# One core, attention inside a gMLP block: the row of score maxima is transposed one step sooner, and its DMA stands one or two steps sooner in the sync queue

## The chip, the cores and the metric

The kernel runs on 1 core of one Trainium2 chip. The metric is the device time of one execution in microseconds (us). A core has a matrix engine (PE, with PEld for its weight loads), a vector engine (DVE), a scalar engine (ACT), GpSimd (POOL) and a sync engine (SP), which here issues nearly all DMAs, in a fixed order.

## What is computed

All data is float32. A pre-norm attention layer with 32 heads of 20 numbers, in which each of 2048 positions sees itself and the 255 before it, is followed by a gMLP block:

```python
def _A_ref(x, wqkv, wo):
    B, S, D = x.shape                       # 1, 2048, 640
    H = 32; Dh = D // H; W = 256
    ...
    scores = jnp.einsum("bhqd,bhkd->bhqk", q, k) * (Dh ** -0.5)
    mask = (idx[:, None] - idx[None, :] >= 0) & (idx[:, None] - idx[None, :] < W)
    scores = jnp.where(mask[None, None], scores, -1e9)
    p = _softmax(scores, axis=-1)
    o = jnp.einsum("bhqk,bhkd->bhqd", p, v)
    return o.transpose(0, 2, 1, 3).reshape(B, S, D) @ wo
def _B_ref(x, w_in, w_sp, b_sp, w_out):
    z = _gelu(x @ w_in); z1 = z[..., :864]; z2 = _layernorm(z[..., 864:])
    g = jnp.einsum("ts,bsf->btf", w_sp, z2) + b_sp[None, :, None]
    return (z1 * g) @ w_out
h  = x + _A_ref(_layernorm(x), A_wqkv, A_wo)
h2 = h + _B_ref(_layernorm(h), B_w_in, B_w_sp, B_b_sp, B_w_out)
```

## The kernel before

The change lies in the attention loop, about 248 to 480 us into the span. Ahead of it stand the first layernorm and the q, k and v products; behind it the output projection and the gMLP block, which reaches to the end.

The 32 heads are eight groups of four, called 0 to 7 here. Queries and keys of a group, split in three bf16 parts, lie in a "stack", a slot of on-chip memory with one row for each part of each of 20 numbers (rows 0 to 119). There are three slots in rotation; their tiles are `slot` and `xb` (`slot_0`, `slot_1`, `xb_0`, `xb_1` for the two halves of the positions). `load_stack` fills a slot from DRAM (`slot<-qk_d`, L279).

The softmax needs the largest score of each query. The kernel works in two passes over the key and query blocks of 128:

- `max_item` (L300 on PE, L312 on DVE) computes the scores of one query block and one head with the query on the partition, and DVE takes the row maximum into a column of `mcol`.
- `score_item` (L366 on PE, L369 on ACT) computes the scores again with the key on the partition, with 123 rows in the product: rows 120 to 122 hold minus the maximum of each query, in three bf16 parts. ACT takes the exponential into `pt`, POOL cuts off the window's edges (L371, L374), and `pv_item` (L394) multiplies by the values. The result leaves PSUM by ACT (L408) or DVE (L410) into `ot`, and SP stores it (`o_d<-ot`, L411).

Between the passes the maxima have to become rows. `max_rows(g, b)` does it for group g and set b, in three pieces. Set 0 is query blocks 0 to 9, set 1 is blocks 10 to 15. The first piece splits the columns in three parts on POOL (L321 to L324, tile `m`). The second multiplies them by minus the identity on PE, which transposes them, and copies the result to `mt` on DVE. The third sends `mt` by DMA to rows 120 to 122 of the group's slot:

```python
            yield
            ps = s1_tile()[:3 * n, :P]
            nc.tensor.matmul(ps, m3.rearrange("p a c -> p (a c)"), minus, start=True, stop=True)   # L330
            mt = tmp2.tile([3 * n, P], BF16, tag="mt", bufs=1, name=f"mt{g}_{b}")
            nc.vector.tensor_copy(mt, ps)                                                          # L332
            yield
            nc.sync.dma_start(st[b][0][120:123], mt.bitcast(F32))                                  # L334
            yield
```

The loop goes over steps s = 0 to 129. A step takes one key block of the score pass, and the maxima of the block 17 places further on (`u1 = s + LEAD`, LEAD = 17), so that the maxima of a group are computed while the scores of the one before are. Within a step the four heads hh = 0 to 3 alternate; `pv_item(s - 2)` has its two halves at hh = 1 and hh = 3. The instructions of PE, DVE and ACT go out in exactly the order in which this code is written; those of SP also, from s = 0 to s = 112. POOL's order, and SP's outside that stretch, is set by a scheduler. Score products of a group begin at u1 % 16 = 1 and read the rows of set 0; those of set 1 are first read eight steps later.

`next(rows)` runs the next piece of `max_rows`. In the kernel before, the first piece stands at u1 % 16 = 10 for set 0 and at 0 for set 1, the second three steps later at hh = 1, and the third at the start of the step two steps after that. SP does nothing but issue DMAs in order, so a DMA stands behind all that were written ahead of it, and waits while one of these waits.

Of the kernel before, what the change touches and what calls it, by code (L numbers as in the profile page):

```python
# [20 lines left out]
NT = S // P  # L21
# [13 lines left out]
def block_kernel(ctx, tc, x, wqk, wv, wo, w_in, wsp, bsp, w_out, out):  # L35
# [5 lines left out]
    def pool(stack, name, **kw):  # L41
        return stack.enter_context(tc.tile_pool(name=name, bufs=1, reuse_waits="tile", **kw))
# [56 lines left out]
    def open_early(pl):  # L99
        mem["t1"] = pl.tile([P, 2 * KF * D], F32R, name="t1")  # L100
        mem["m1"] = pl.tile([P, 6 * D + 4 * P], F32, name="m1")
        mem["xh"] = [pl.tile([P, D], F32, name=f"xh{i}") for i in range(2)]
        mem["ho"] = [pl.tile([P, D], F32, name=f"ho{i}") for i in range(3)]
        mem["wraw"] = pl.tile([P, 2, 2, HF], F32, name="wraw")
# [55 lines left out]
    def proj_o(i, ps):  # L160
        osp = ots.pop(i)
        wo_s = t1(0, 2, KD, D)
        gemm(ps, HD, [lambda k, p=p: osp[:, p, k, :] for p in range(2)],
             [lambda k, j, p=p: wo_s[:, p, k, j * HD:(j + 1) * HD] for p in range(2)], KD)
        return ps
# [35 lines left out]
    with ExitStack() as ab:  # L201
# [43 lines left out]
        NU = 128  # L245
# [22 lines left out]
        def load_stack(g):  # L268


            st = slot_w[g % 3]
            if g < 3:
                for h in st:
                    nc.gpsimd.memset(h[1][96:P], ONES)
            for c in range(2):
                for j, parts in enumerate(((0, 0), (0, 1), (0, 2), (1, 0), (1, 1), (2, 0))):
                    for a in range(2):
                        src = qk_d[c][a][g // 4, parts[a], :, g % 4 * 4:g % 4 * 4 + 4]
                        nc.sync.dma_start(st[c][a][j:6 * DH:6], src)  # L279
                        yield  # L280
# [6 lines left out]
        def max_item(g, qb, hh, strips=True):  # L287

            st, half = slot_ap[g % 3], qb // 8
            ps = s1_tile()  # L290
            lo = max(0, qb - 2) * P
            n = (qb + 1) * P - lo
            keep = mask[:, 384 - n:]
            if strips:
                skip = 32 if qb > 1 else 0
                if skip:
                    n, keep = 288, strip
                for j in range(4):
                    q0 = qb * P + 32 * j
                    nc.tensor.matmul(ps[32 * j:32 * j + 32, :n], part(st, half, 120, 0, hh, q0, 32),  # L300
                                     part(st, half, 120, 1, hh, lo + skip * j, n),
                                     start=True, stop=True, tile_position=(0, 32 * j))
            else:
                nc.tensor.matmul(ps[:, :n], part(st, half, 120, 0, hh, qb * P, P), part(st, half, 120, 1, hh, lo, n),
                                 start=True, stop=True)
            b, c = (0, qb) if qb < 10 else (1, qb - 8)
            r = (10, 8)[b]
            if c == 2 * b and hh == 0:
                m_cols[b] = tmp2.tile([P, 4 * r], F32, tag=f"mcol{b}", bufs=1, name=f"mcol{g}_{b}")
            junk = tmp2.tile([P, 384], BF16, tag="junk", bufs=2, name=f"junk{g}_{qb}_{hh}")  # L310
            c += hh * r
            nc.vector.tensor_tensor_reduce(out=junk[:, :n], in0=ps[:, :n], in1=keep, scale=1.0,  # L312
                                           scalar=NEG, op0=OP.add, op1=OP.max, accum_out=m_cols[b][:, c:c + 1])

        def max_rows(g, b):


            n, cols, st = (40, 32)[b], m_cols.pop(b), slot_w[g % 3]
            m3 = tmp2.tile([P, 3, n], BF16, tag="m3", bufs=1, name=f"m3_{g}_{b}")
            mr = tmp2.tile([P, n], F32, tag="mr", bufs=1, name=f"mr{g}_{b}")  # L320
            nc.gpsimd.tensor_copy(out=m3[:, 0], in_=cols)  # L321
            nc.gpsimd.tensor_tensor(out=mr, in0=cols, in1=m3[:, 0], op=OP.subtract)
            nc.gpsimd.tensor_copy(out=m3[:, 1], in_=mr)
            nc.gpsimd.tensor_tensor(out=m3[:, 2], in0=mr, in1=m3[:, 1], op=OP.subtract)  # L324
            if b == 0:
                nc.gpsimd.tensor_copy(out=m_cols[1].rearrange("p (h r) -> p h r", h=4)[:, :, :2],
                                      in_=cols.rearrange("p (h r) -> p h r", h=4)[:, :, 8:])
# [8 lines that stand above are left out]
# [17 lines left out]
        def score_item(u, hh):  # L353


            g, kb = divmod(u, NT)
            st = slot_ap[g % 3]
            n = min(384, S - kb * P)
            if hh == 0:
                p_tiles[u] = tmp3.tile([P, 4, 384], F32, tag="pt", bufs=4, name=f"pt{u}")  # L360
            pt = p_tiles[u]
            ps = s2_tile()
            for i in range(4):
                k0, half = kb * P + 32 * i, kb // 8
                b, e = 32 * i, min(n, 32 * i + 288)
                nc.tensor.matmul(ps[32 * i:32 * i + 32, b:e], part(st, half, 123, 1, hh, k0, 32),  # L366
                                 part(st, half, 123, 0, hh, kb * P + b, e - b),
                                 start=True, stop=True, tile_position=(0, 32 * i))
            nc.scalar.activation(pt[:, hh, :n], ps[:, :n], AF.Exp, scale=SCALE)  # L369
            if hh == 3:  # L370
                nc.gpsimd.affine_select(out=pt[:, :, :P], in_=pt[:, :, :P], pattern=[[0, 4], [1, P]], base=0,  # L371
                                        channel_multiplier=-1, compare_op=OP.is_ge, fill=0.0)
                if n == 384:
                    nc.gpsimd.affine_select(out=pt[:, :, 256:], in_=pt[:, :, 256:], pattern=[[0, 4], [-1, P]],  # L374
                                            base=-1, channel_multiplier=1, compare_op=OP.is_ge, fill=0.0)
# [233 lines left out]
        for s in range(NU + 2):  # L609
            if s % NT == 0 and s < 6 * NT:  # L610
                ld = load_stack(s // NT + 2)
            u1 = s + LEAD
            if u1 <= NU + 5 and u1 % NT in (5, 15):
                next(rows)
            for _ in range(1 + s % 2):
                next(ld, None)
            for hh in range(4):
                if u1 < NU:
                    max_item(u1 // NT, u1 % NT, hh)
                if s < NU:  # L620
                    score_item(s, hh)
                if hh == 0 and u1 <= NU and u1 % NT in (0, 10):
                    rows = max_rows((u1 - 1) // NT, 0 if u1 % NT else 1)
                    next(rows)
                if hh == 1 and u1 <= NU + 3 and u1 % NT in (3, 13):
                    next(rows)
                if hh == 2 + s - NU and s >= NU:
                    if s == NU:
                        psB.close()
                        psW = pool(psB, "psW", space=PSUM)  # L630
                    pre_ps.append(proj_o(s - NU, psW.tile([P, 2, 512], F32, tag="wo", bufs=3, name=f"wo_ps{s - NU}")))
                if s >= 2:
                    if hh == 1:
                        pv = pv_item(s - 2)
                        next(pv, None)
                    if hh == 3:
                        next(pv, None)
            if u1 == NU:
                ring[2].append(ring[1].pop(0))
            if s == NU - NT:  # L640
                sync.close()
                low0.close()
                lowx.close()
                open_early(pool(early_stack, "early"))
                early = proj_early()
            if early is not None and s > NU - NT:
                next(early, None)
            for f in inverse:
                next(f, None)
# [566 lines left out]
```

## Time and profile before

| | |
|---|---|
| median of 3 runs | 1154.88 us (1151.7 to 1155.35) |
| the profiled execution | 1156.74 us, span 1154.3 us, mean granted clock 0.99 |
| PE busy | 1098.6 us (95% of the span), 10652 instructions |
| DVE, ACT, POOL busy | 746.3, 535.8, 406.1 us |
| chain that ended last | PE 31%, DVE 5%, POOL 2% of the span |
| L330, L332, L334 | 16 of each; medians 257, 286 and 757 ns |

The profile is one execution. PE is busy in almost the whole span, so what counts is where it is idle and what ended that. In rows of the timeline the columns are start (us from the span's start), length (us), engine, line, operation, tiles and count; behind them in brackets the idle time before, with what ended it. SP is written SPq there. A row of the waits gives the waiting engine, its tile and line, what it waited for, and the sum in us, the number and the longest. Window rows give, for each stretch, its length and the busy us of each engine with the number of its instructions, then the granted clock, the DMA engines' busy share and GB/s.

### The profile page before, as it was taken

What the parts mean: (1) busy time and instruction counts of PE and PEld (TensorE: products, weight loads), DVE (VectorE), ACT (ScalarE), POOL (GpSimd) and SP (SyncE); (2) the same over time, 40 slices, a digit from 0 to 9 for tenths busy, and PEclk for the clock granted to TensorE, in tenths of its full rate; (3) what the DMA queues carried; (4) which work ended last, traced back from release to release, by engine and by line L of the source; (5) the groups of instructions that cost most, each with busy time, mean ns of one, the idle gap of its engine ahead of it and who ended that gap; (6) DMA issues with size and microseconds to landing.
All of it is one profiled execution on the core that took longest, in us unless ns stands there. A gap on an engine that the chain in (4) does not pass through costs nothing. (4 is left out here: it accounts for less than half of the span.)

```text
span 1154.3 us, 27630 instructions
## 1 busy us (share of the span) xinstructions
PE 1098.6 (95%) x10652; PEld 982.7 (85%) x10652; DVE 746.3 (65%) x1963; ACT 535.8 (46%) x1165; POOL 406.1 (35%) x553
## 2 busy tenths in 40 slices
PE   6999999999999999889999998999999899999998
PEld 6998876667777776588999997999999799999998
DVE  5541113788999996789868489555548974655443
ACT  3333333258888889534356555333335421222210
POOL 4124444556667667656421065000116520000000
PEclk9999999999999999999999998999999999999999
DMA  6213565655666644487745412133341463444322
GB/s 194 69 35 98 169 209 173 213 182 185 192 193 199 192 155 147 151 256 269 255 143 206 157 50 74 68 120 131 103 137 52 145 199 135 133 144 133 97 80 81
DMA packets 83844, 170.84 MB, mean 148 GB/s; under 512 B 11008, under 2 KB 47360, under 8 KB 79872
## 3 DMA queue, kind: packets, MB, share of 16 engines
q1 hardware_dynamic: 81408, 163.83, 44.0%
q10 hardware_dynamic: 2304, 5.24, 1.2%
q8 instruction: 83, 1.36, 0.5%
q14 instruction: 49, 0.40, 0.1%
HBM read 112.37 MB, written 56.23 MB: 146 GB/s over the span
## 5 line engine op out<-in xcount | busy, mean ns | idle before, releaser
L369 ACT ACTIVATE pt<-bank 128x384 f32<-128x384 f32 (+2 forms) x512 | 201.6, 499 | 25.6 <-PE bank L300 11.6
L1013 PE MATMUL g<-zl,aw 128*128 128x432 f32 x768 | 174.5, 362 | 7.3 <-ACT zl L681 5.0
L681 ACT ACTIVATE aw<-fx 128x512 fp32r<-128x512 f32 (+2 forms) x160 | 92.8, 595 | 189.8 <-PE g L1013 124.2
L312 DVE CUSTOM_DVE_ANT_0 junk<-bank,strip 128x288 bf16<-128x288 f32 x392 | 157.4, 454 | 7.7 <-PE bank L300 5.2
L1013 PEld LDWEIGHTS g<-zl,aw 128*128 128x128 f32 x768 | 144.8, 189 | 16.2 <-ACT zl L681 5.9
L1013 PE MATMUL g<-ze,aw 128*128 128x432 f32 x576 | 138.1, 368 | 4.7 <-DVE row L675 2.4
L675 DVE TENSOR_TENSOR aw<-fx,aw 128x512 fp32r<-128x512 f32 (+2 forms) x152 | 107.8, 718 | 37.6 <-ACT aw L681 37.2
L394 PE MATMUL pv<-pt,v_sb 128*32 128x192 f32 (+3 forms) x1984 | 126.9, 323 | 2.4 <-POOL pt L371 1.9
L1013 PEld LDWEIGHTS g<-ze,aw 128*128 128x128 f32 x576 | 109.3, 192 | 12.6 <-DVE row L675 1.9
L366 PE MATMUL bank<-slot 123*32 123x288 bf16 (+6 forms) x1536 | 108.0, 283 | 10.3 <-DMA slot<-mt 8.7
L371 POOL TENSOR_SCALAR_AFFINE_SELECT pt<-pt 128x512 f32<-128x512 f32 x128 | 84.0, 657 | 60.2 <-ACT pt L369 59.7
L1052 PE MATMUL out_ps<-wout,y_sp 128*128 128x320 f32 (+1 forms) x630 | 96.2, 309 | 0.4 <-ACT y_sp L124 0.4
L1052 PEld LDWEIGHTS out_ps<-wout,y_sp 128*128 128x128 f32 (+1 forms) x630 | 94.1, 188 | 1.3 <-ACT y_sp L124 0.7
L917 PE MATMUL zb<-win,aw 128*128 128x432 f32 x480 | 95.2, 359 | 0.0
L917 PEld LDWEIGHTS zb<-win,aw 128*128 128x128 f32 x480 | 90.0, 188 | 4.5
L300 PE MATMUL bank<-slot 120*32 120x288 bf16 (+2 forms) x1264 | 88.3, 283 | 0.5 <-issue 0.5
L498 DVE TENSOR_TENSOR rest<-qk,sg 128x512 f32<-128x512 f32 x40 | 27.7, 692 | 86.9 <-ACT sg L496 86.8
L366 PEld LDWEIGHTS <-slot 123*32 123x32 bf16 x1536 | 53.0, 97 | 29.0 <-DMA slot<-mt 10.4
L501 POOL TENSOR_TENSOR sg<-rest,sg 128x512 bf16<-128x512 f32 x40 | 46.6, 1164 | 73.6 <-ACT sg L500 70.5
L374 POOL TENSOR_SCALAR_AFFINE_SELECT pt<-pt 128x512 f32<-128x512 f32 x112 | 72.3, 645 | 0.0
L675 DVE TENSOR_TENSOR row<-g,row 128x432 f32<-128x432 f32 x80 | 48.0, 603 | 36.7 <-PE g L1013 32.8
L394 PEld LDWEIGHTS pv<-pt,v_sb 128*32 128x32 f32 x1984 | 59.7, 110 | 8.4 <-POOL pt L371 3.8
(189 smaller groups left out, 2173.4 us busy)
## 6 DMA issues: line engine op xcount, KB each, us to landing
fx<-wsp_in SPq DMA_DIRECT2D x32, 512.0 KB
slot<-qk_d SPq DMA_DIRECT2D x72, 200.0 KB
qk_d<-sg SPq DMA_DIRECT2D x32, 384.0 KB
slot<-qk_d SPq DMA_DIRECT2D x72, 160.0 KB
fx<-hn_d SPq DMA_DIRECT2D x32, 320.0 KB
o_d<-ot SPq DMA_DIRECT2D x64, 128.0 KB
z_d<-row SPq DMA_DIRECT2D x16, 432.0 KB
g_d<-row SPq DMA_DIRECT2D x16, 432.0 KB
```

The source lines that it names most:

```text
L300: nc.tensor.matmul(ps[32 * j:32 * j + 32, :n], part(st, half, 120, 0, hh, q0, 32), part(st, half, 120, 1, hh, lo + skip * j, n), start=Tru ...
L312: nc.vector.tensor_tensor_reduce(out=junk[:, :n], in0=ps[:, :n], in1=keep, scale=1.0, scalar=NEG, op0=OP.add, op1=OP.max, accum_out=m_cols ...
L366: nc.tensor.matmul(ps[32 * i:32 * i + 32, b:e], part(st, half, 123, 1, hh, k0, 32), part(st, half, 123, 0, hh, kb * P + b, e - b), start=T ...
L369: nc.scalar.activation(pt[:, hh, :n], ps[:, :n], AF.Exp, scale=SCALE)
L371: nc.gpsimd.affine_select(out=pt[:, :, :P], in_=pt[:, :, :P], pattern=[[0, 4], [1, P]], base=0, channel_multiplier=-1, compare_op=OP.is_ge ...
L374: nc.gpsimd.affine_select(out=pt[:, :, 256:], in_=pt[:, :, 256:], pattern=[[0, 4], [-1, P]], base=-1, channel_multiplier=1, compare_op=OP. ...
L394: nc.tensor.matmul(ps[32 * hh:32 * hh + 32, a - 512 * c:b - 512 * c], v_sb[:, kb, v0:v0 + 32], pt[:, hh, a - kb * P:b - kb * P], start=fir ...
L675: (eng or nc.vector).tensor_tensor(out=out, in0=a, in1=b, op=op)
L681: nc.scalar.activation(out, a, AF.Copy)
L917: nc.tensor.matmul(b[0][:, :HF], a[t][:, x, kk], win2[0][:, y, kk, h * HF:(h + 1) * HF], start=kk + x + y == 0, stop=kk == KD - 1 and x == 1)
L1013: nc.tensor.matmul(ps, w[m][:, x, k], zc[k][m][:, y], start=start and k + x + y == 0, stop=stop and k == 3 and x == 1, skip_group_check=True)
L1052: nc.tensor.matmul(ps[j][:, :HD], src[:w, a, k, :], e1["wout"][:w, b, k, j * HD:(j + 1) * HD], start=(k == 0 and a + b == 0), stop=(k == K ...
```

## The change

The second piece of `max_rows` moves one step forward for both sets, from u1 % 16 = 13 and 3 to 12 and 2. The third moves from 15 to 13 for set 0 (two steps) and from 5 to 4 for set 1 (one step). The first piece stays. Group 0's set 0 is handled ahead of the loop by other code that is not changed.

```diff
             u1 = s + LEAD
-            if u1 <= NU + 5 and u1 % NT in (5, 15):
+            if u1 <= NU + 4 and u1 % NT in (4, 13):
                 next(rows)
             for _ in range(1 + s % 2):
                 next(ld, None)
...
                 if hh == 0 and u1 <= NU and u1 % NT in (0, 10):
                     rows = max_rows((u1 - 1) // NT, 0 if u1 % NT else 1)
                     next(rows)
-                if hh == 1 and u1 <= NU + 3 and u1 % NT in (3, 13):
+                if hh == 1 and u1 <= NU + 2 and u1 % NT in (2, 12):
                     next(rows)
```

What this does to the order of instructions is shown for group 4 and its set 0; groups 1 to 3, 5 and 6 are alike, and in group 7 there are no loads of slots any more. Names carry the group, as `m3_4_0` (parts of group 4, set 0), `mt4_0`, `slot1_0` (its slot). `pt57` and `pt58` are the exponentials of steps 57 and 58, two steps back.

SP before, where the rows of group 4 are sent:

```order
L411 DMA o_d_66<-ot3_1_1_5807 128x256
L279 DMA xb1_95<-qk_d10_64 20x2048
L279 DMA xb1_95<-qk_d11_65 20x2560
L279 DMA xb1_95<-qk_d10_64 20x2048
L411 DMA o_d_66<-ot3_2_0_5959 128x256
L334 DMA slot1_0_1917<-mt4_0_5867 3x40x64
```

SP now, at the same place:

```order
L411 DMA o_d_66<-ot3_1_1_5810 128x256
L334 DMA slot1_0_1917<-mt4_0_5808 3x40x64
L279 DMA xb1_95<-qk_d10_64 20x2048
L279 DMA xb1_95<-qk_d11_65 20x2560
L279 DMA xb1_95<-qk_d10_64 20x2048
L411 DMA o_d_66<-ot3_2_0_5960 128x256
```

The rows' DMA has moved ahead of three loads of a later group's slot and of the store of `ot3_2_0`, and stands right behind the store of `ot3_1_1`.

PE before, around the transposing product (weights and product, L330):

```order
L366 LDWEIGHTS slot0_1_100
L366 MATMUL bank3_121<-slot0_1_100 32x288
L330 LDWEIGHTS m3_4_0_5673
L330 MATMUL bank1_119<-minus_110,m3_4_0_5673 120x128
L394 MATMUL pv3_2_5653<-pt58_5733,v_sb_112 32x256 x4
```

PE now:

```order
L366 LDWEIGHTS slot0_1_100
L366 MATMUL bank5_123<-slot0_1_100 32x288
L330 LDWEIGHTS m3_4_0_5673
L330 MATMUL bank2_120<-minus_110,m3_4_0_5673 120x128
L394 MATMUL pv3_2_5653<-pt57_5667,v_sb_112 32x192 x4
```

It now stands ahead of the value product of `pt57` instead of that of `pt58`, one step sooner.

DVE before, from the maximum of block 12, head 1 to the copy of the transposed rows (L332):

```order
L312 ISA junk4_12_1_5800,mcol4_1_5664<-bank0_118,strip_109 128x288
L312 ISA mcol4_1_5664 128x1
L410 COPY ot3_1_1_5807<-pv3_1_5420 128x256
L312 ISA junk4_12_2_5818,mcol4_1_5664<-bank2_120,strip_109 128x288
L312 ISA mcol4_1_5664 128x1
L312 ISA junk4_12_3_5829,mcol4_1_5664<-bank1_119,strip_109 128x288
L312 ISA mcol4_1_5664 128x1
L312 ISA junk4_13_0_5847,mcol4_1_5664<-bank0_118,strip_109 128x288
L312 ISA mcol4_1_5664 128x1
L312 ISA junk4_13_1_5859,mcol4_1_5664<-bank2_120,strip_109 128x288
L312 ISA mcol4_1_5664 128x1
L332 CAST mt4_0_5867<-bank1_119 120x128
```

DVE now:

```order
L312 ISA junk4_12_1_5800,mcol4_1_5664<-bank0_118,strip_109 128x288
L312 ISA mcol4_1_5664 128x1
L332 CAST mt4_0_5808<-bank2_120 120x128
L410 COPY ot3_1_1_5810<-pv3_1_5420 128x256
L312 ISA junk4_12_2_5821,mcol4_1_5664<-bank1_119,strip_109 128x288
```

The copy has moved ahead of the copy of `ot3_1_1`. POOL keeps its order in the whole loop. It is the same before and now at the place that matters, with the third part of the maxima (L324) between the two edge cuts of `pt57`:

```order
L323 CAST m3_4_0_5673<-mr4_0_5674 128x40
L371 AFFINE_SELECT pt57_5667<-pt57_5667 128x4x128
L324 TENSOR_TENSOR m3_4_0_5673<-mr4_0_5674,m3_4_0_5673 128x40
L374 AFFINE_SELECT pt57_5667<-pt57_5667 128x4x128
L371 AFFINE_SELECT pt58_5733<-pt58_5733 128x4x128
```

Two things move that the diff doesn't name. Around the start of the loop, two loads of group 2's slot go behind the rows of group 0's set 1 instead of ahead of those of its set 0. And in the output projection behind the loop, where a scheduler sets the order, some ten instructions of each engine change places: transposes of h on PE move by about 13 products, and on DVE the normalisations (L148) and the sums of h (L1160) are interleaved otherwise. No instruction is added or removed anywhere.

## The prediction

> **What bounds the kernel now.** I read the waits of PE first, since PE is busy in 95% of the span and only its idle time can be won; then the timeline at each of those waits; then the other engines there, to see whether one of them would take over. In the list of PE's waits two rows belong to the rows of maxima (sum in us, number, longest):
>
> ```profile
> PE bank L366 <- DMA slot<-mt: 8.7, 5, 2.0
> ...
> PE bank L366 <- DMA xb<-mt: 1.4, 1, 1.4
> ```
>
> The score product waits six times, 10.1 us in all, for the DMA that sends the maxima. The timeline says where:
>
> ```profile
> 276.70 0.31 PE L366 MATMUL bank<-slot 123*32 123x288 bf16 x4 [1.94 <-DMA slot<-mt]
> 303.98 0.30 PE L300 MATMUL bank<-xb 120*32 120x288 bf16 x2 [1.08 <-issue]
> 336.01 0.31 PE L366 MATMUL bank<-slot 123*32 123x288 bf16 x4 [1.95 <-DMA slot<-mt]
> 364.59 0.31 PE L366 MATMUL bank<-slot 123*32 123x288 bf16 x4 [1.57 <-DMA slot<-mt]
> 393.88 0.31 PE L366 MATMUL bank<-xb 123*32 123x288 bf16 x4 [1.43 <-DMA xb<-mt]
> 423.09 0.31 PE L366 MATMUL bank<-slot 123*32 123x288 bf16 x4 [1.51 <-DMA slot<-mt]
> 451.69 0.43 PE L366 MATMUL bank<-slot 123*32 123x288 bf16 x8 [1.74 <-DMA slot<-mt]
> ```
>
> They lie some 29 us apart, one at the first score product of each of groups 1 and 3 to 7: set 0 is late each time. Group 2 (about 306) has none, since PE had lost 1.08 us to something else just before, and the rows caught up. Set 1 never makes PE wait: its rows are read eight steps later.
>
> Idle PE is worth something only if the others are idle too. At group 4 and group 7 the rows are
>
> ```profile
> 365.06 0.42 DVE L312 CUSTOM_DVE_ANT_0 junk<-bank,mask 128x256 bf16<-128x256 f32 x1 [1.45 <-PE bank L300]
> 365.03 2.40 ACT L369 ACTIVATE pt<-bank 128x384 f32<-128x384 f32 x6 [2.09 <-PE bank L300]
> 452.12 8.54 ACT L369 ACTIVATE pt<-bank 128x384 f32<-128x384 f32 x22 [2.17 <-PE bank L366]
> ```
>
> DVE and ACT run dry with PE, so the whole loop stands still. From one set-0 transposition to the next (length; busy us of PE, PEld, DVE, ACT, POOL), the first and the sum of six:
>
> ```profile
> 268.69:299.34 30.65, 28.32 (x766) 23.02 (x762) 27.03 (x135) 26.29 (x69) 20.01 (x40) 0.94 0.58 188
> ...
> sum 175.39, PE 163.45 PEld 133.10 DVE 159.32 ACT 155.42 POOL 120.37; mean PE 27.24 PEld 22.18 DVE 26.55 ACT 25.90 POOL 20.06
> ```
>
> In these 175.39 us PE is idle 11.9 and DVE 16.1. The five waits among them are 8.4 us. Without them DVE still has 7.7 us to spare, 1.3 us a group: near to being the bound, not yet the bound.
>
> **Why the rows are late, and what the change does.** Group 4, all on the way of its set 0:
>
> ```profile
> 354.37 0.26 POOL L324 TENSOR_TENSOR m<-mr,m 128x40 bf16<-128x40 f32 x1
> 354.58 0.63 POOL L374 TENSOR_SCALAR_AFFINE_SELECT pt<-pt 128x512 f32<-128x512 f32 x1
> ...
> 355.12 0.51 PE L394 MATMUL pv<-pt,v_sb 128*32 128x192 f32 x8
> ...
> 356.96 0.25 PE L330 MATMUL bank<-minus,m 128*120 128x128 bf16 x1
> ...
> 355.74 0.42 DVE L410 COPY ot<-pv 128x256 f32<-128x256 f32 x1
> ...
> 357.58 0.29 DVE L332 CAST mt<-bank 120x128 bf16<-120x128 f32 x1
> ...
> 360.37 0.42 ACT L408 ACTIVATE ot<-pv 128x256 f32<-128x256 f32 x1
> ...
> 354.13 2.24 SPq L279 DMA_DIRECT2D xb<-qk_d  x3
> 356.47 0.41 SPq L411 DMA_DIRECT2D o_d<-ot  x1
> 356.93 2.24 SPq L279 DMA_DIRECT2D xb<-qk_d  x3
> 360.81 0.33 SPq L411 DMA_DIRECT2D o_d<-ot  x1
> 361.24 0.76 SPq L334 DMA_DIRECT2D slot<-mt  x1
> ```
>
> The rows are ready in `mt` at 357.87, but SP sends them at 361.24: in its order they stand behind three loads and behind the store of `ot3_2_0`, which ACT makes only at 360.37. So 3.4 us are lost in the queue, and the PE wait is 1.57.
>
> *Third piece, set 0, two steps.* Now the rows stand behind the store of `ot3_1_1` alone. The transposition comes ahead of the value product at 355.12, 1.84 us sooner than 356.96. DVE is busy until 355.74; there the copy takes 0.29, and the copy of `ot3_1_1` starts at 356.03 instead of 355.74. Its store followed 0.73 us after that start (356.47), so now at 356.76; the DMA after a store follows 0.46 later (356.93 after 356.47): the rows go out at 357.2, 4.0 us sooner. From issue to the product it was 364.59 - 361.24 = 3.35 us, so they land at about 360.6. PE comes there at 364.59 - 1.57 = 363.0. The wait goes, with 2.4 us to spare. The tightest place might be group 7, where the loop is about to change its pace:
>
> ```profile
> 441.61 0.26 POOL L324 TENSOR_TENSOR m<-mr,m 128x40 bf16<-128x40 f32 x1
> ...
> 442.24 0.51 PE L394 MATMUL pv<-pt,v_sb 128*32 128x192 f32 x8
> ...
> 442.86 0.42 DVE L410 COPY ot<-pv 128x256 f32<-128x256 f32 x1
> ...
> 448.35 0.75 SPq L334 DMA_DIRECT2D slot<-mt  x1
> ```
>
> 442.86 + 0.29 + 0.73 + 0.46 = 444.3, and with 451.69 - 448.35 = 3.34 us landed at 447.7; PE comes at 449.95. 2.3 us to spare. The term: 1.94 + 0 + 1.95 + 1.57 + 1.43 + 1.51 + 1.74 = 10.1 us. Its ends: nothing, if the rows stay late; 13 us, if ACT's longer pauses (2.09 against PE's 1.57, 0.5 more in each of six) count. I take PE's own, because PE has the least idle time.
>
> *Second piece, one step.* Same product, same copy, so no busy time is added. PE now needs the third part (L324) sooner: ready at 354.63 for 355.12 (0.49 us to spare), in group 7 at 441.87 for 442.24 (0.37). More than that, the value product right behind it reads `pt57`, and POOL finishes `pt57` (L374) behind L324; if POOL is late, PE stood there before as well. I take 0; if the margin failed by 0.26, one L324, in 15 places, 4 us.
>
> *What falls back on SP.* Three loads go out one DMA later (0.76 us) and the store of `ot3_2_0` is no later, since it waits for ACT. The loads fill a slot that is used a group later: 0. *Third piece, set 1:* it passes two loads and a store; nobody waited for these rows: 0. *Group 0:* two loads change places with the first rows; 2.24 / 3 = 0.75 us each, so 1.5 us either way; I take 0.
>
> *Output projection.* Its reordered stretch is
>
> ```profile
> 480.00:520.00 40.00, 35.13 (x226) 33.55 (x227) 33.42 (x51) 12.69 (x23) 20.02 (x20) 0.92 0.74 227
> 520.00:560.00 40.00, 37.04 (x250) 36.23 (x249) 39.50 (x67) 16.66 (x29) 26.49 (x26) 0.96 0.83 287
> ...
> PE wo_ps L91 <- DVE xh L1160: 4.7, 2, 2.8
> PE wo_ps L91 <- DVE t L154: 2.6, 1, 2.6
> ```
>
> PE is idle 7.8 us there and DVE full in the second half. The same work in another order can't be priced from the trace; one such wait more or less is 2.8 us, and I take 0 between -2.8 and +2.8.
>
> *The clock.* After group 1's wait the granted clock was half for some 3 us:
>
> ```profile
> 278.00:279.00 1.00, 1.00 (x30) 0.77 (x24) 0.76 (x5) 0.78 (x3) 0.15 (x1) 0.50 0.52 162
> 279.00:280.00 1.00, 1.00 (x24) 0.83 (x20) 0.68 (x4) 0.93 (x3) 1.00 (x2) 0.50 0.59 207
> 280.00:281.00 1.00, 1.00 (x24) 0.72 (x20) 0.85 (x4) 0.93 (x3) 0.07 (x1) 0.50 0.53 166
> ...
> 326.00:327.00 1.00, 1.00 (x37) 0.91 (x33) 0.98 (x5) 1.00 (x4) 0.90 (x3) 1.00 0.70 178
> ```
>
> 78 products in 3 us instead of 37 a us: 0.9 us lost. After none of the other five waits does the clock drop, so I don't count it; if it goes with the wait, the gain is 11.0. The Trainium skill ("TensorE: Matmul & The Clock Gate", Part 1) says that the clock falls to half after an idle window of about 3.4 us. No wait here is that long; by that rule the drop isn't the wait's doing and the gain stays 10.1, and five of the six waits agree.
>
> **The sum.** 10.1 us off the profiled execution: 1156.74 - 10.1 = 1146.6 us. The median of the runs stands 1.86 us below the profiled one, so 1154.88 - 10.1 = 1144.8, about 1145 us (0.9% faster). A measurement here tells 0.3%, 3.5 us, from no change.
>
> **Rivals.**
> A. *Rows still late, behind the loads.* In its old place the rows' DMA is issued 2.07 us after the last load was (359.17 to 361.24), now 0.8 us after (356.37 to 357.2). If the loads are still draining then, up to 1.3 us come on top, and the rows land at 361.9: still 1.1 us before PE. It decides from 2.4 us on. For it speaks that loads and stores run all through the loop (188 GB/s in group 1's row); against it, the sum above. If half of the waits stay, 1150. The Trainium skill ("DMA: Bandwidth & Descriptors", the section on why a DMA increments its semaphore by 16) says that a transfer is spread over the largest number of engines up to 16 that divides its rows: 10 for these loads of 20 rows. A busy share of 0.58 of 16 engines would then mean that the loads' engines are nearly full, and this is why A has more than a small chance.
> B. *The time comes back.* DVE has 1.3 us a group left, or the chain at the head of the projection (the 2.6 us for `t`) runs on DMAs and not on PE. Then most of the 10 us turns into other waits: about 1154. Against it: DVE and ACT were idle in the very same microseconds.
> C. *Slower: the transposition becomes the wait.* The product now stands ahead of a value product on PE, and its copy ahead of DVE's maxima. If POOL's parts come late, both engines halt, and behind them ACT. To end 3.5 us above before, 10.1 + 3.5 = 13.6 us must be lost in 15 places, 0.9 us each, so that L324 would end 1.4 us later against PE than in group 4. Time: 1159 or more. Against it: POOL is busy 20.06 of 29.2 us a group, and L374 behind it gated PE already.
>
> **How the numbers follow.** As forecast (1142 to 1148): 0.72. A: 0.15, mostly still over 0.3% faster. B: 0.07. C, or the reordered projection at its worst: 0.06. Faster 0.84, same 0.10, slower 0.06. The range goes from 1141 (11.0 from the waits and clock and 2.8 from the projection) to 1151 (half of the waits kept, and a little more).
>
> **What would show it.** Right: no wait of L366 for `mt`; groups of about 27.5 us instead of 29.2; the rows' issue right behind the store of `ot3_1_1`, 4 us ahead of the old place. Wrong: waits of L366 for `mt` under 1 us in most groups (A); new waits of PE for DVE's `mcol`, or a longer one for `t` at the projection's head (B); a wait of L330 for L324, with L332 idle behind it (C).

## Result: 1.0% faster, and the profile after

| | before | after |
|---|---|---|
| median of 9 runs | 1154.88 us (1151.7 to 1157.59) | 1144.05 us (1139.77 to 1148.88) |
| ratio, 95% interval | | 0.9902 (0.9881 to 0.9924) |
| the profiled execution | 1156.74 us, span 1154.3 | 1147.21 us, span 1144.7 |

The forecast was 1145.0 us, between 1141 and 1151. In the list of PE's waits of the changed kernel, the rows of L366, and two others that come up later, are these (waiting tile and line, what it waited for, sum in us, number, longest):

```profile
PE wo_ps L91 <- DVE t L154: 4.1, 1, 4.1
...
PE ht_ps L806 <- DVE m L81: 1.7, 2, 1.0
...
PE bank L366 <- issue: 1.6, 4, 0.5
...
PE bank L366 <- ACT pt L369: 1.1, 2, 0.9
```

No row with `mt` is left, where it was 8.7 + 1.4 us before. The timeline of SP at group 4 shows why (start, length, engine, line, tiles, count):

```profile
346.51 0.33 SPq L411 DMA_DIRECT2D o_d<-ot  x1
346.88 2.24 SPq L279 DMA_DIRECT2D xb<-qk_d  x3
349.22 0.42 SPq L411 DMA_DIRECT2D o_d<-ot  x1
349.69 0.76 SPq L334 DMA_DIRECT2D slot<-mt  x1
350.48 2.25 SPq L279 DMA_DIRECT2D xb<-qk_d  x3
353.51 0.33 SPq L411 DMA_DIRECT2D o_d<-ot  x1
```

The rows go out right behind a store, 0.47 us after it. The next store, behind which they stood before, is issued at 353.51: 3.8 us later. The transposition on the way there (POOL, PEld, PE and DVE):

```profile
347.12 0.26 POOL L324 TENSOR_TENSOR m<-mr,m 128x40 bf16<-128x40 f32 x1
347.98 0.13 PEld L330 LDWEIGHTS <-m 128*120 128x120 bf16 x1 [0.19 <-POOL pt L374]
347.98 0.27 PE L330 MATMUL bank<-minus,m 128*120 128x128 bf16 x1
348.48 0.29 DVE L332 CAST mt<-bank 120x128 bf16<-120x128 f32 x1
348.69 0.41 DVE L410 COPY ot<-pv 128x256 f32<-128x256 f32 x1
```

PEld waited 0.19 us at the product, and the copy of `ot` follows DVE's copy of `mt`. From one set-0 transposition to the next, the six stretches together and the first of them are now (length, then the busy us of PE, PEld, DVE, ACT, POOL, the granted clock, the DMA share and GB/s):

```profile
265.81:293.00 27.19, 26.72 (x767) 22.03 (x763) 26.31 (x135) 25.82 (x70) 20.06 (x39) 1.00 0.64 209
...
sum 164.96, PE 160.91 PEld 133.31 DVE 158.41 ACT 154.96 POOL 120.25; mean PE 26.82 PEld 22.22 DVE 26.40 ACT 25.83 POOL 20.04
```

164.96 us against 175.39, or 27.5 us a group against 29.2. DVE's work is the same (158.4 against 159.3 us), but it fills 96% of the stretch, not 91%.

### The profile page after: what moved, and what is told of

It is laid out like the page before. It is cut to its first block, busy times and chain, and to the rows that moved or that the text cites. A ratio compares the mean times of both kernels' runs of the same rounds, so it can differ in the third digit from the quotient of the medians.

```text
span 1144.7 us, 27633 instructions
## 1 busy us (share of the span) xinstructions
PE 1096.0 (96%) x10652; PEld 983.2 (86%) x10652; DVE 746.7 (65%) x1963; ACT 535.8 (47%) x1165; POOL 405.5 (35%) x553
## 5 line engine op out<-in xcount | busy, mean ns | idle before, releaser
L366 PE MATMUL bank<-slot 123*32 123x288 bf16 (+6 forms) x1536 | 107.0, 282 | 2.1 <-ACT pt L369 1.1
L374 POOL TENSOR_SCALAR_AFFINE_SELECT pt<-pt 128x512 f32<-128x512 f32 x112 | 72.3, 645 | 0.0
L366 PEld LDWEIGHTS <-slot 123*32 123x32 bf16 x1536 | 52.6, 97 | 17.2 <-issue 6.0
```

## Experiments

The change has two pieces and two sets, and one question lies under it: what held the rows back in SP's queue? "One step" is one s of the loop. All kernels were timed in five rounds against the kernel before; in the three groups of runs in which they were timed, that kernel had medians of 1155.69, 1154.55 and 1155.05 us. Diffs are against the kernel before where nothing else is said.

### The second piece alone, the third piece alone

Transposition one step sooner for both sets, DMA left in its place:

```diff
-                if hh == 1 and u1 <= NU + 3 and u1 % NT in (3, 13):
+                if hh == 1 and u1 <= NU + 2 and u1 % NT in (2, 12):
```

> Only the transposing product and its copy move one step sooner (both sets); the DMA of the rows stays at its old place. Theory Q (the rows are late because of their place in SP's order): they are sent behind three loads and behind the store of ot of step 13 as before, so the six waits of the score product on mt stay at about 10 us in all and the time at 1155 us (within 3). Rival T (the rows are late because they are made late, and the sooner product is what helps): waits gone, about 1145 us.

Measured: 1154.94 us (1151.81 to 1161.78), ratio 0.9999 (0.9982 to 1.0016). Nothing. Its waits of PE, the copy to `mt` of group 4, and SP where the rows go out:

```profile
PE bank L366 <- DMA slot<-mt: 9.5, 5, 2.5
...
PE bank L366 <- DMA xb<-mt: 3.0, 2, 1.7
```

```profile
354.21 0.28 DVE L332 CAST mt<-bank 120x128 bf16<-120x128 f32 x1
...
359.23 0.33 SPq L411 DMA_DIRECT2D o_d<-ot  x1
359.60 0.76 SPq L334 DMA_DIRECT2D slot<-mt  x1
```

`mt` is complete at 354.49, and for 5.1 us nothing is done with it: the rows still go out behind the store. A piece that is ready earlier in front of an unmoved DMA only waits longer. (The seven waits add up to 12.5 us here, against 10.1 in six before, at the same median time: sums of waits of single executions differ by that much.)

The DMA of set 0 one step sooner, and the transposition left in its place:

```diff
-            if u1 <= NU + 5 and u1 % NT in (5, 15):
+            if u1 <= NU + 5 and u1 % NT in (5, 14):
```

> Only the DMA of the rows of set 0 moves, one step sooner (u1 % 16 = 14 for 15); the transposing product stays late. Theory Q: in SP's order the DMA now stands behind one load, ahead of two and of the store; in group 4 it would be sent at about 358.0 us, when the copy to mt ends (357.87), instead of 361.24, and land at 361.3, ahead of PE at 363.0; the waits on mt go and the time is 1144 to 1147 us. Rival T: the product is as late as before, so most of the gain is missing: 1150 us or more.

Measured: 1143.38 us (1141.19 to 1145.49), ratio 0.9894 (0.9876 to 0.9912): the whole gain. In its list of PE's waits no row of L366 has `mt`, and the rows now go out as soon as they exist, behind one load instead of three and ahead of the late store:

```profile
351.48 0.29 DVE L332 CAST mt<-bank 120x128 bf16<-120x128 f32 x1
...
350.38 0.41 SPq L411 DMA_DIRECT2D o_d<-ot  x1
350.83 0.72 SPq L279 DMA_DIRECT2D xb<-qk_d  x1
351.79 0.77 SPq L334 DMA_DIRECT2D slot<-mt  x1
```

`mt` is complete at 351.77 and the DMA is issued at 351.79.

### One set alone

```diff
-            if u1 <= NU + 5 and u1 % NT in (5, 15):
+            if u1 <= NU + 5 and u1 % NT in (5, 13):
...
-                if hh == 1 and u1 <= NU + 3 and u1 % NT in (3, 13):
+                if hh == 1 and u1 <= NU + 3 and u1 % NT in (3, 12):
```

> Both moves for set 0 alone (12 and 13); set 1 as before. The order of SP at the head of the loop is then that of the kernel before. Theory Q: all of the gain, 1144 to 1147 us, and no wait on mt. Rival E (a part comes from what moved elsewhere: the two loads at the head of the loop or the output projection): 1148 us or more.

Measured: 1143.96 us (1142.03 to 1146.49), ratio 0.9897 (0.9877 to 0.9918). With set 1 alone, `NU + 4` with `(4, 15)` for the DMA and `NU + 2` with `(2, 13)` for the product:

> Both moves for set 1 alone (2 and 4); set 0 as before. Theory Q: nobody waited for these rows, so the six waits on mt stay at about 10 us and the time at 1155 us (within 3). Rival E: some us faster, up to the part that set 0 alone leaves.

Measured: 1154.11 us (1151.74 to 1158.01), ratio 0.999 (0.9975 to 1.0005), with the waits of before and one more, 12.0 us in seven:

```profile
PE bank L366 <- DMA slot<-mt: 8.8, 5, 2.1
...
PE bank L366 <- DMA xb<-mt: 3.2, 2, 1.9
```

Set 1 is worth nothing, as nobody waited for its rows.

### One step later

```diff
-            if u1 <= NU + 5 and u1 % NT in (5, 15):
+            if u1 <= NU + 5 and u1 % NT in (5, 0):
```

> The kernel before, with the DMA of the rows of set 0 one step later still (u1 % 16 = 0 for 15), which is one load of 0.75 us more ahead of it in SP's order. Theory Q: each wait grows by about 0.8 us, in seven groups, so 1155 + 5 to 6 = 1160 to 1161 us, and the waits on mt come to about 16 us. Rival: the lateness is hidden elsewhere and the time stays at 1155. On the clock: with waits of some 2.5 us in each group the rule of an idle window of 3.4 us still lets none of them drop the clock; if the waits drop it by chance as in group 1 of the first profile, two or more groups show a granted clock of 0.94 and the time is 1 to 3 us longer.

Measured: 1170.42 us (1168.65 to 1172.74), ratio 1.0139 (1.0118 to 1.0161): 15.9 us slower, about three times what was expected. The waits of PE:

```profile
PE bank L366 <- DMA slot<-mt: 14.9, 5, 3.8
...
PE bank L366 <- DMA xb<-mt: 6.0, 2, 3.2
```

20.9 us against 10.1 are 10.8 us of the 15.9. The rows are sent 4.1 to 4.3 us after the copy to `mt` in groups 1 to 6, where it was 3.4 to 3.5 before: that is the one load more, as expected. But right behind it they also take 3.8 to 4.8 us from issue to product in these groups, where it was 3.2 to 3.7. The rest is, by the estimate below, the clock. The timeline at three of the waits, and two of the 1-us windows behind the middle one:

```profile
278.26 0.39 PE L366 MATMUL bank<-slot 123*32 123x288 bf16 x4 [2.64 <-DMA slot<-mt]
...
309.31 0.43 PE L366 MATMUL bank<-xb 123*32 123x288 bf16 x4 [2.79 <-DMA xb<-mt]
...
341.43 0.43 PE L366 MATMUL bank<-slot 123*32 123x288 bf16 x4 [3.71 <-DMA slot<-mt]
```

```profile
309.00:310.00 1.00, 0.69 (x16) 0.50 (x20) 0.00 (x0) 0.12 (x1) 0.00 (x0) 0.54 0.59 211
...
312.00:313.00 1.00, 1.00 (x32) 0.79 (x28) 0.75 (x3) 0.72 (x3) 0.65 (x2) 0.76 0.42 160
```

Between them it is 0.50. So the granted clock is half from 309.08 to 312.48, for 3.4 us, and likewise after each of the six waits of 2.64 to 3.78 us, and also after the seventh, 1.74 us in group 7. After the two longest it is half for 6.8 us, and PE works in 5 to 6 of them. With 24 to 28 products in a us instead of some 37, that is an estimated 0.9 us lost after four of the six and 1.5 after two, 6.6 us in all, of which before had 0.9. 10.8 + 5.7 = 16.5 us, near the 15.9.

### What holds the rows: the store or the loads

Set 0's rows stood behind three loads and a store. This kernel puts them between the two, at the end of the step ahead of the old place, without moving anything else:

```diff
-            if u1 <= NU + 5 and u1 % NT in (5, 15):
+            if u1 <= NU + 5 and u1 % NT == 5:
                 next(rows)
...
+                if hh == 3 and u1 <= NU and u1 % NT == 14:
+                    next(rows)
```

> The kernel before, with the DMA of the rows of set 0 moved past one thing only: it stands ahead of the store of ot of step 13 and still behind all three loads (written at hh = 3 of the step u1 % 16 = 14). Theory S (the store is what holds SP, since ACT makes its tile late; the loads only cost their issue time): in group 4 the rows would be sent at about 359.2 us, when the third load is out, instead of 361.24, and land at 362.5, ahead of PE at 363.0; waits on mt under 2 us in all, 1144 to 1147 us. Rival L (the loads hold the rows, in SP's order or because their data are still being moved when the rows come): the rows land 3 us or more after the loads' last packets, waits of 0.5 to 1.5 us stay in most groups, 1148 to 1155 us.

Measured: 1150.56 us (1146.5 to 1154.75), ratio 0.9961 (0.9945 to 0.9977): some 40% of the gain. DVE, SP and PE in group 4 (the profiled execution was the slowest of the ten):

```profile
355.37 0.29 DVE L332 CAST mt<-bank 120x128 bf16<-120x128 f32 x1
...
354.72 2.24 SPq L279 DMA_DIRECT2D xb<-qk_d  x3
357.06 0.76 SPq L334 DMA_DIRECT2D slot<-mt  x1
358.60 0.33 SPq L411 DMA_DIRECT2D o_d<-ot  x1
```

```profile
362.52 0.31 PE L366 MATMUL bank<-slot 123*32 123x288 bf16 x4 [1.71 <-DMA slot<-mt]
```

The rows are sent 1.5 us ahead of the store and no longer wait for ACT, but still 1.4 us after they are ready (355.66), since the loads are issued first. And from issue to product it now takes 362.52 - 357.06 = 5.46 us, where it was 3.35 in the kernel before, and PE still waits 1.71. In the six groups of this kernel in which PE waited it was 3.75 to 5.46 us. So part of the store's delay had been hiding a second one: right behind loads, the rows' own data come later. The traces also record every packet that a DMA moves, which no view shown here does; the rows are the only packets of 256 bytes in the loop, 120 of them for set 0. The last one ended 3.0 to 4.6 us after the issue in groups 1 to 6 of this kernel and 2.0 to 3.0 in the kernel before. In group 7, where no slot is loaded any more, it was 2.0 us in both.

Two kernels test the loads and the store apart. The first takes two of the three loads from ahead of the rows and leaves the rows in that place (the other line is as in the diff above):

```diff
-            for _ in range(1 + s % 2):
+            for _ in range({13: 0, 14: 2, 15: 3}.get(s % NT, 1 + s % 2)):
```

> As pre_store (the rows of set 0 ahead of the store of ot of step 13), and the two loads of step s % 16 = 13 are issued one and two steps later, behind the rows, so that one load instead of three stands just ahead of them. In pre_store the rows were sent 0.1 us after the third load and took 3.75 to 5.5 us from issue to the first score product, against 3.2 to 3.7 in the kernel before. Theory L (the loads' data, still moving, hold the rows' data): sent when the copy to mt ends, with 3 to 4 us from issue to product, no waits on mt, 1144 to 1146 us. Rival (what was left in pre_store has another cause, such as the rows' place within the step): 1150 us as there.

Measured: 1145.05 us (1141.74 to 1148.28), ratio 0.9903 (0.9873 to 0.9934). No row of L366 among PE's waits has `mt`. DVE and SP in group 4:

```profile
351.62 0.28 DVE L332 CAST mt<-bank 120x128 bf16<-120x128 f32 x1
...
350.97 0.73 SPq L279 DMA_DIRECT2D xb<-qk_d  x1
351.93 0.77 SPq L334 DMA_DIRECT2D slot<-mt  x1
354.85 0.33 SPq L411 DMA_DIRECT2D o_d<-ot  x1
```

The rows are ready at 351.90 and are sent at 351.93. Over groups 1 to 6 they are sent 0.1 us after the copy on average, and in pre_store 1.7. Their packets came hardly sooner: the last one 3.1 to 4.0 us after the issue, 3.5 on average against 3.9. So what pre_store lacked was mostly the time that SP spends issuing two loads, some 0.75 us each, and only to a small part the moving of their data.

The second leaves the rows where they were before, behind the store, and takes the loads away:

```diff
-            for _ in range(1 + s % 2):
+            for _ in range({11: 2, 12: 0, 13: 0, 14: 3, 15: 3}.get(s % NT, 1 + s % 2)):
```

> The kernel before, with the rows at their old place behind the store of ot of step 13, but the three loads of steps 12 and 13 issued two steps later, behind the rows; only the two stores stand just ahead of them. Theory S (the store alone holds SP until ACT has made its tile): the rows are sent as late as before (361.2 us in group 4, some 3.4 us after the copy to mt), the time from issue to product falls to 2.5 to 3.3 us since no loads are in front, and waits of 0.5 to 1.5 us stay in most groups: 1149 to 1155 us. Rival (the loads alone were the cause): no waits, 1145 us.

Measured: 1153.08 us (1150.55 to 1157.46), ratio 0.9983 (0.9965 to 1.0001). DVE, ACT, SP and PE in group 4:

```profile
357.87 0.28 DVE L332 CAST mt<-bank 120x128 bf16<-120x128 f32 x1
...
360.65 0.41 ACT L408 ACTIVATE ot<-pv 128x256 f32<-128x256 f32 x1
...
356.76 4.66 SPq L411 DMA_DIRECT2D o_d<-ot  x2
361.51 0.77 SPq L334 DMA_DIRECT2D slot<-mt  x1
...
365.15 0.31 PE L366 MATMUL bank<-slot 123*32 123x288 bf16 x4 [1.84 <-DMA slot<-mt]
```

Nothing but the two stores is ahead now, and SP sits in them until ACT has made `ot`: the rows are ready at 358.15 and are sent at 361.51, 3.4 us later, just as in the kernel before. So the store alone takes the gain away, and the loads alone more than half of it: gap_pre (no store, and one load that is out before the rows are ready) has the gain, pre_store (three loads) has part, and gap_post (store) none that is clear of noise.

### The time that came back

At the head of the output projection PE waits 4.1 us for `t` in the changed kernel, 2.6 before. `t` hangs on the reciprocals of the softmax's sums, in front of which DVE stands in the changed kernel:

```profile
466.53 0.95 DVE L348 RECIPROCAL inv<-inv 128x128 f32<-128x128 f32 x1 [7.02 <-DMA inv<-o_d]
```

DVE works in order, so for 7.0 us it waits there for the DMA that fetches the sums and does nothing else. This kernel is the changed one, with that reciprocal written later, behind other work of DVE:

```diff
     (in inverse_sums, against the changed kernel)
-            yield
-            yield
+            for _ in range(6 if c == 1 else 2):
+                yield
```

> The changed kernel, and the reciprocal of the second quarter's sums is given to DVE four steps later, behind the normalisation and the split of the first two tiles of the projection. In the changed kernel DVE waits 7 us in that reciprocal, in order, for sums that come back by DMA, and PE's first product of the projection waits 4.1 us for t behind it. Theory P: that wait falls under 1.5 us and the time is 2 to 3 us below the changed kernel, about 1141 to 1142 us. Rival: the next tile or the later quarters wait instead, about 1144 us.

Measured: 1146.29 us (1144.28 to 1147.9), against before 0.9927 (0.9911 to 0.9944), so no faster than the changed kernel. Its PE waits in the projection (460 to 560 us):

```profile
PE ht_ps L806 <- DVE m L81: 7.0, 6, 2.4
PE wo_ps L91 <- DVE mvc L76: 3.4, 2, 2.2
...
PE wo_ps L91 <- DVE t L154: 1.0, 1, 1.0
```

The wait for `t` fell by 3.1 us, and that for `xh` (L1160) from 6.3 in the changed kernel to 0.5. But the one for `m` rose from 1.7 to 7.0, and one for `mvc` and one of 1.7 us for ACT appeared. The order that shortens some waits of PE there lengthens others: DVE waits only 2.7 us for these sums now, where it was 8.8, but no time was won by it.

## Why the prediction was right, point by point

- *The six waits, 10.1 us.* Right: the waits are gone, and the median of the runs fell by 10.8 us. That the two numbers lie so close is partly luck. In the profiled executions the loop, from its first product to its last, took 11.7 us less (218.7 us against 230.4); it began 1.7 us sooner, and 3.8 us were given back behind it (see B): 9.6 in all. Of what the loop won above 10.1, some 0.9 is the clock: the half clock after group 1's wait is gone with the wait (1.00 in the row from 265.81). The prediction named it and left it out. The rest, 0.7 us, is not accounted for. (The six stretches are 175.39 - 164.96 = 10.43 us shorter, but they hold five of the waits, 8.4 us; the sixth lies behind them.)
- *The rows go out 4.0 us sooner, in 3.35 us.* The first half is right: 0.47 us behind the store, ready 0.9 us earlier. The second half was luckier than it looks. The rows had 355.57 - 349.69 = 5.88 us there until the group's first score product:

```profile
355.57 0.30 PE L366 MATMUL bank<-slot 123*32 123x288 bf16 x4
```

  Where nobody waits, the views don't show how long the rows took. But three loads ended 0.57 us before, and the records of packets show their effect: the last of the rows' 120 packets ended 3.45 us after the issue, at 353.14, where it was 2.00 in the kernel before. In the runs in which PE waited for the rows, the product followed the last packet after 0.5 to 1.6 us. So of the "2.4 us to spare" 0.8 to 1.9 were left in this group.
- *Rival A, the loads.* Its mechanism is real, and its size was about right for the changed kernel: "up to 1.3 us on top" against 3.45 - 2.00 = 1.45 us in group 4. In pre_store it was more, 5.46 - 3.35 = 2.1 us. In the changed kernel it stays hidden, because the rows go out 4 us sooner. The Trainium skill ("DMA: Bandwidth & Descriptors", the section on why a DMA increments its semaphore by 16) has the loads of 20 rows on 10 of 16 engines; a DMA share of 0.64 of 16 in the row from 265.81, just above 10 / 16 = 0.63, is near what full engines of that number would give, but the row holds stores as well as loads, so it proves nothing. The runs show that the rows' packets come later behind loads (2.0 us in group 7, up to 4.6 in pre_store); that the rows queue on those very engines no run here shows.
- *Second piece, 0.* Right: t_only gives 0.9999, and the margins of 0.49 and 0.37 us were enough. But the prediction joined both pieces into one path and did not say which of them was needed. d_only says it: the third piece alone, one step, brings all.
- *Set 1, 0.* Right: set1 gives 0.999 (0.9975 to 1.0005), set0 the full gain.
- *Output projection, 0 +- 2.8, and rival B.* B happened on a small scale, if at all. The first L91 product of the changed kernel:

```profile
469.07 7.22 PE L91 MATMUL wo_ps<-t 128*128 128x320 f32 x30 [4.09 <-DVE t L154]
```

  So PE left the loop at 469.07 - 4.09 = 464.98, and 679.7 us follow in a span of 1144.7. In the kernel before that product starts at 481.02 after a wait of 2.62 us: PE left the loop at 478.40, and 675.9 us follow. So 3.8 us were given back: 1.5 at `t`, 1.3 in the rest of the projection, whose last products start 10.6 us sooner (557.49 against 568.09), and 1.0 in the gMLP block. For the projection that is just the stated end of 2.8. But in the nine kernels of the experiments it was 674.2 to 678.3 us from the loop to the end, one execution each, and the loop began between 246.9 and 248.6 us. So most of the 3.8, and of the 1.7 us ahead of the loop, may be scatter.
- *C, the transposition as the wait.* Did not occur. At L330 PEld waited for POOL six times, 1.2 us in all, and PE's product never waited for L324 or L374.
- *The clock and the rule.* The prediction set a rule of 3.4 us (the Trainium skill, "TensorE: Matmul & The Clock Gate", Part 1) against the drop after a wait of 1.94 us, and took the drop not to be the wait's doing. That step was wrong: in late0 the clock fell after each of seven waits, five of them shorter than 3.4 us, and in set1 after both waits of 2.08 us. The same part says that the window runs freely, and late0 agrees: read off 1-us rows, its clock falls at 278.36, 309.08, 339.80, 373.93, 408.06, 438.78 and 469.50, always 9 or 10 times 3.41 us apart, and it stays at half for 3.4 or 6.8 us. So the run has a fixed grid of 3.41 us, and what matters is how little PE does between two of its marks, not how long it waits without a break. The kernel before at group 1, and t_only, whose grid follows from a drop at 476.72, at a wait of 2.49 us:

```profile
274.28:277.69 3.41, 1.47 (x48) 0.95 (x40) 1.46 (x9) 0.93 (x4) 1.57 (x5) 1.00 0.63 180
277.69:281.11 3.42, 3.42 (x72) 2.66 (x68) 2.65 (x13) 3.06 (x8) 1.22 (x2) 0.50 0.53 173
```

```profile
277.27 0.31 PE L366 MATMUL bank<-slot 123*32 123x288 bf16 x4 [2.49 <-DMA slot<-mt]
...
271.92:275.33 3.41, 2.86 (x100) 2.19 (x92) 3.41 (x21) 2.62 (x10) 2.62 (x8) 1.00 0.56 177
275.33:278.75 3.42, 1.48 (x52) 1.33 (x53) 0.91 (x7) 1.04 (x3) 0.72 (x2) 1.00 0.63 183
```

  The wait of 1.94 us lies whole between two marks, PE is busy for 1.47 us of 3.41 there, and half clock follows. The wait of 2.49 us is cut by a mark into 0.55 and 1.94, PE is busy for 2.86 and 1.48, and none follows. In the loops of before, t_only, set1, pre_store, gap_post and late0 the clock fell after all nine such stretches with up to 1.47 us of busy PE, and otherwise only after the seventh wait of late0 (1.60). So against the rule a stretch need not be idle as a whole, and the measurement decides. Since two stretches with 1.48 and 1.54 us passed without, busy time alone doesn't set the limit, and what does is open.

## What to carry to other kernels

Where a small DMA is late, compare three times: when its data are ready, when the queue issues it, and when its reader starts; the first gap is work queued ahead of it that may itself be waiting for an engine (3.4 us here), the second grows with the loads just issued ahead of it (from 3.35 up to 5.46 us in group 4). Move the DMA, not the work that makes its data, when the first gap isn't zero: one line, one step and one set of the two brought everything. Margins for such a move are to be counted with the longest time from issue to landing that can occur in the new place, not with the one seen in the old place.

## What was not expected of the hardware

- One and the same DMA, the maxima's rows of group 4, took 3.35 us from issue to product where a store that waited stood between it and the loads, and 5.46 us right behind three loads of the same queue. Its last packet ended 2.0 us after the issue in the first place, 4.2 in the second, and 3.6 in gap_pre, behind one load.
- The granted clock of PE changed only at marks 3.41 us apart. Waits of 2.64 to 3.78 us were followed by half clock six times out of six, and shorter ones where they fell whole between two marks and left PE busy for at most 1.47 us there. In late0 that added about half as much again to what the waits themselves cost (an estimated 5.7 us to 10.8), so that the same step taken backwards costs more (15.9 us) than it brings forwards (11 us).
- Not settled: whether the part behind the loop really gives some of the gain back (3.8 us in one execution). PE's wait for `t`, 4.1 us in the changed kernel, was 2.9 and 2.7 in d_only and set0, which have the same gain. Moving DVE's reciprocals only moved the waits, and no version tried is clearly faster than the changed kernel; the intervals of d_only and set0 overlap its own.
